# Retention and SwiGLU on one core: the first pair of heads by 128 tokens, products of the identity ahead of it, a new order of the first loads, and keys of pairs five to eight loaded once

## The chip, the core and the metric

The kernel runs on one core of a Trainium2 chip. The time is in device microseconds (us), from the start of the program on the core to its end; smaller is better. A "profiled execution" is one execution that the hardware profiler recorded; its span is what the trace covers, and its own time is what the same clock as in the timed runs gave for it.

The engines are TensorE (PE; its weight loads are listed apart as PEld), VectorE (DVE), ScalarE (ACT), GpSimd (POOL) and SyncE (SP), which here only issues transfers. Sixteen DMA engines move the data.

## The reference

```python
# attention: q, k, v are (8 batches, 8 heads, 576 tokens, 64) in float32
scores = scale * q @ k.T                       # scale = 1 / sqrt(64)
gamma  = 1 - 2 ** (-5 - head)
ret    = scores * where(i >= j, gamma ** (i - j), 0)     # i: query, j: key
attn   = ret @ v
# bridge: (8, 8, 576, 64) -> x of (4608 tokens, 512)
# feed-forward: the three weights are float64
g   = x @ w_gate                               # (512, 1536)
val = x @ w_val                                # (512, 1536)
out = (g * sigmoid(g) * val) @ w_out           # (1536, 512)
```

The result is float32, 4608 by 512.

## The kernel before

**Retention.** Two heads make a pair, and each batch has four pairs, so there are 32 pairs; the text counts them from 1, the code from 0 (`HP` is 4, so pairs 1 to 4 are `i < HP`, the first batch). A pair's 576 tokens are nine chunks of 64. Inside a chunk the scores are computed and masked (scores, L573; mask `near`, L580); from chunk to chunk a 64x64 state is carried: `new_states` (L543) multiplies scaled keys by values, and the states of the chunks are summed with decays on VectorE: pairs of chunks (L596), odd chunks (L603), even chunks (L608), after ScalarE has copied the even states out of PSUM (`copies`, L584). `own_values` (L532) multiplies values by the masked scores; `earlier_values` (L559) adds queries times states; `to_x` (L640 and L645) copies the sum into `x`, the input of the feed-forward part. On the first four pairs only eight of the nine chunks are done; the ninth chunks of the four pairs are done together later (`end_loads`, `end_scores` and the others with `end_`).

Queries and keys are needed with the head's dimension on the partitions. In the first four pairs TensorE transposes them (L466), four 128x128 blocks each, into PSUM, and ScalarE (VectorE for pair 1) copies them to `qT` and `kT` (L470 to L473). From pair 5 on, q and k come by columns in four transfers each (L282) into 32-row strips, and one 32x32 transposition by VectorE (L492) finishes the work; k is loaded a second time by tokens (L287 to L291) for the states. Keys are scaled in `keys` (L505 or L507); queries of pairs 2 to 4 by GpSimd in `scale_run` (L735).

**Feed-forward.** The first 512 tokens are computed plainly: for each of twelve hidden blocks of 128, `up0` (L842 to L857) adds four 512-column products (one for each 128 rows of `x`, "input blocks", that is, for each pair) for the gate and four for the value, ScalarE takes silu (L856), VectorE multiplies (L857); then `down0` (L864) adds four 512-column products for each hidden block. Hidden blocks use the banks A and B, or C and E, in turn. The rest of the tokens go through a scheme with fewer products (L1186, L1392), with sums of operands on VectorE and GpSimd; it fills the time after 172 us.

**Weights.** They come as float64 and are made float32 in the kernel: `load_w` brings 256 columns, 1 MB (for the first four transfers' worth as four pieces of 256 KB each, L370; later in one transfer), ScalarE splits the bits of a half (`split`, L389 and L390) and VectorE rounds and packs them (`rounding`, L406 and L407). The first five transfers are issued on SyncE, the later ones on ScalarE. A raw buffer is free when its two halves have been split, and `split` then issues the next load; the fifth load is held until a fixed place.

**Order.** On the five engines the order of the instructions is that of the program (`manual_schedule`, L1425). The first batch is written as six calls of `tick(t, 0, HP)` (L1427): each brings transposes of pair t, scores and states of the pair before, and own and earlier values of the pair before that. TensorE's sequence from 20 us on is: transposes of pair 4, own and earlier values of pair 3, hidden block 0 with input blocks 0 and 1 (four products), scores and states of pair 4, hidden block 1 with input blocks 0 and 1, own and earlier values of pair 4, and then hidden blocks 0 and 1 with input blocks 2 and 3 (L1434). After that a `plan` (L1450 to L1480) mixes the hidden blocks 2 to 11 with the rounding of weights (`round_until`), loads of pairs, and the ticks of pairs 5 to 10: `tick(4)` stands ahead of hidden block 2, `tick(5)` behind block 3, and the next ones behind blocks 5, 7, 10 and 11. The pieces of a tick on VectorE, ScalarE and GpSimd are put in a list, `pieces`, and drained by `go_on`.

SyncE issues, in order: the small part of a table of decays (`tab[:, 0:NCOL]`, L311), q, k and v of pairs 1 and 2 (shared with ScalarE), pair 3, the large part of the table (L337), pair 4, then the first two weights' pieces, the third and the fourth, each in 256 KB pieces; pair 5 and the fifth weight follow from within the ticks.

## Time and profile before

| | |
|---|---|
| timed runs | 1015.04, 1016.25, 1018.67 us; median 1016.25 |
| profiled execution, its own time | 1014.55 us |
| its span in the trace | 1012.8 us |
| TensorE busy in the span | 1000.9 us (99%) |
| VectorE, GpSimd, ScalarE busy | 710.9, 561.8, 286.7 us |
| moved by DMA | 194.38 MB in 278,892 packets |
| end of TensorE's last product | 1009.4 us |
| first transpose of pair 4 on TensorE | 20.54 us |
| hidden blocks 0 and 1 begin their third input block | 33.98 us |
| end of the plain down products, about | 172 us |

All times of the trace are counted from the start of the span. A group in the timeline is a run of like instructions without a gap: start, busy time, engine, line, operation, out and in, shape and count; in brackets the engine's idle time before it and what ended that. One float32 product or transpose of 128 columns or more can appear as two records, and some records are missing, so counts are not exact. Busy times in the listings include the overlap of neighbouring instructions; the step from one start to the next is the price of one in a dense sequence.

### The profile page before, as it was taken

How to read it: one execution, taken by the hardware profiler on the slowest of the kernel's cores; microseconds unless marked ns; L12 is line 12 of the kernel's file. 1: busy time of each engine (PE TensorE's matmuls, PEld its weight loads, DVE VectorE, ACT ScalarE, POOL GpSimd, SP SyncE). 2: the span in 40 equal slices, each digit the busy share in tenths (PEclk: the TensorE clock that was granted, in tenths of full speed). 3: DMA queues.
4: the chain of work that ended last, by engine and by line, in shares of the span. 5: the costliest groups of instructions: out<-in, count | busy, mean ns of one | idle time of the engine just before them, and what ended most of it. 6: DMA issues, size and time to landing. Idle time of an engine off the chain costs nothing.

```text
span 1012.8 us, 21319 instructions
## 1 busy us (share of the span) xinstructions
PE 1000.9 (99%) x8336; PEld 825.5 (82%) x8336; DVE 710.9 (70%) x1206; ACT 286.7 (28%) x636; POOL 561.8 (55%) x589
## 2 busy tenths in 40 slices
PE   6999999999999999999999999999999999999998
PEld 5655555888888888888888888888888888888887
DVE  4488887677875766977777678866575767566645
ACT  4565522132423312133422202233220012232110
POOL 3400359979375228575564157746672586566514
PEclk9999999999999999999999999999999999999999
DMA  9999866967587787647677777434454554445553
GB/s 245 261 288 272 192 216 234 264 193 214 138 238 207 217 231 193 198 156 196 184 202 206 198 179 217 154 133 159 161 172 141 154 189 147 148 155 180 182 159 102
DMA packets 278892, 194.38 MB, mean 192 GB/s; under 512 B 212552, under 2 KB 246088, under 8 KB 278792
## 3 DMA queue, kind: packets, MB, share of 16 engines
q1 hardware_dynamic: 251464, 94.70, 36.7%
q10 hardware_dynamic: 26688, 97.92, 29.1%
q8 instruction: 66, 1.08, 0.5%
q0 software_dynamic: 640, 0.39, 0.2%
q14 instruction: 34, 0.28, 0.1%
HBM read 154.04 MB, written 38.93 MB: 191 GB/s over the span
## 4 chain that ended last, share of the span: by engine, by line
PE 94%; DVE 2%; DMA 1%; POOL 1%; SPq 0%; issue 0%; ACT 0%; DVEq 0%; ACTq 0%; POOLq 0%
PE bankB L1186 12%; PE bankC L1186 11%; PE bankA L1186 11%; PE bankE L1186 11%; PE bankB L1392 7%; PE bankC L1392 7%; PE bankE L1392 6%; PE bankA L1392 6%; PE outer L532 2%; PE bankE L853 2%; PE bankA L853 2%; PE outer L1186 2%; PE inner L1186 2%; PE bankB L853 2%; PE outer L559 2%; PE bankC L853 2%
## 5 line engine op out<-in xcount | busy, mean ns | idle before, releaser
L1042 POOL TENSOR_TENSOR rest<-rest 128x512 f32<-128x512 f32 (+1 forms) x139 | 148.0, 1076 | 159.9 <-DVE rest L1042 112.5
L1201 POOL TENSOR_TENSOR arena<-rest,io 128x256 f32<-128x256 f32 x168 | 123.9, 750 | 89.4 <-ACT io L1200 88.9
L1200 ACT ACTIVATE io<-rest 128x256 f32<-128x256 f32 x192 | 79.3, 417 | 200.0 <-DVE rest L1042 140.0
L1186 PE MATMUL bankB<-rest,arena 128*128 128x256 f32 x448 | 114.5, 380 | 0.0
L1042 DVE TENSOR_TENSOR rest<-bankB,rest 128x512 f32<-128x512 f32 x116 | 78.5, 685 | 40.5 <-PE bankB L1186 28.5
L1186 PE MATMUL bankC<-rest,arena 128*128 128x256 f32 x416 | 106.3, 380 | 0.0
L1186 PE MATMUL bankA<-rest,arena 128*128 128x256 f32 x412 | 104.8, 379 | 0.0
L1042 DVE TENSOR_TENSOR rest<-bankA,rest 128x512 f32<-128x512 f32 x111 | 75.2, 685 | 40.8 <-PE bankA L1186 19.3
L1042 DVE TENSOR_TENSOR rest<-bankC,rest 128x512 f32<-128x512 f32 x110 | 74.5, 683 | 38.0 <-PE bankC L1186 23.4
L1042 DVE TENSOR_TENSOR rest<-bankE,rest 128x512 f32<-128x512 f32 x106 | 71.7, 684 | 36.2 <-PE bankE L1186 17.6
L1186 PE MATMUL bankE<-rest,arena 128*128 128x256 f32 x372 | 94.9, 380 | 0.3 <-DVE rest L1042 0.3
L1186 PEld LDWEIGHTS bankB<-rest,arena 128*128 128x128 f32 x448 | 84.7, 190 | 11.9 <-DVE rest L1042 0.2
L1186 PEld LDWEIGHTS bankC<-rest,arena 128*128 128x128 f32 x416 | 78.5, 190 | 11.4 <-DVE rest L1042 0.8
L1186 PEld LDWEIGHTS bankA<-rest,arena 128*128 128x128 f32 x412 | 78.1, 190 | 10.9 <-DVE rest L1042 0.2
L1186 PEld LDWEIGHTS bankE<-rest,arena 128*128 128x128 f32 x372 | 70.3, 190 | 10.4 <-DVE rest L1042 0.8
L1042 POOL TENSOR_TENSOR arena<-arena 128x256 f32<-128x256 f32 (+1 forms) x76 | 70.3, 947 | 11.1 <-PE bankC L1186 9.0
L886 POOL TENSOR_TENSOR rest<-rest 128x512 f32<-128x512 f32 x21 | 28.5, 1377 | 72.1 <-DVE rest L407 58.5
L1392 PE MATMUL bankB<-arena 128*128 128x256 f32 x264 | 61.0, 381 | 0.0
L1392 PE MATMUL bankE<-arena 128*128 128x256 f32 x264 | 60.8, 380 | 0.0
L1392 PEld LDWEIGHTS bankE<-arena 128*128 128x128 f32 x264 | 50.0, 190 | 6.9
L1392 PEld LDWEIGHTS bankB<-arena 128*128 128x128 f32 x264 | 49.8, 190 | 6.9
L1392 PE MATMUL bankC<-arena 128*128 128x256 f32 x240 | 55.2, 379 | 0.0
(270 smaller groups left out, 1876.0 us busy)
## 6 DMA issues: line engine op xcount, KB each, us to landing
arena<-up ACTq DMA_DIRECT2D x63, 896.0 KB, 4.6
arena<-dn ACTq DMA_DIRECT2D x65, 384.0 KB, 3.1
arena<-dn SPq DMA_DIRECT2D x39, 384.0 KB, 3.1
out_dram<-rest SPq DMA_DIRECT2D x31, 256.0 KB, 3.4
qk<-in_q_dram SPq DMA_DIRECT2D x108, 72.0 KB, 3.1
qk<-in_k_dram SPq DMA_DIRECT2D x108, 72.0 KB, 3.4
dn<-rest SPq DMA_DIRECT2D x26, 256.0 KB, 2.8
up<-arena SPq DMA_DIRECT2D x13, 512.0 KB, 5.6
```

Of the source, the lines that this page charges most:

```text
L532: m = nc.tensor.matmul(value(i, hl, c), s["v"][rows, at], ret[rows, c % 2 if whole(i) else hl, c // 2], start=start, stop=start, skip_grou ...
L559: nc.tensor.matmul(xr[half[hl]] if c + 1 == NC else value(i, hl, c), state[half[hl], c, :], s["qT"][half[hl], ts(c, L)], start=False, stop ...
L853: nc.tensor.matmul(bank, w, xs[0][:, c, :], start=(c == 0), stop=(c == HP - 1))
L886: eng.tensor_tensor(out=dst, in0=srcs[0], in1=srcs[1], op=ALU.add if op[0] == "add" else ALU.subtract)
L1042: eng.tensor_tensor(out=out, in0=a, in1=b, op=ALU.add if sign > 0 else ALU.subtract)
L1186: m = nc.tensor.matmul(b[:, g * TB : (g + 1) * TB], w[:, g], x, start=(opens and g == 0), stop=True, skip_group_check=True)
L1200: nc.scalar.activation(out=s, in_=src[:, 0:TB], func=AF.Silu)
L1201: (nc.vector if busy and o != 2 and qd + 1 < NQ else nc.gpsimd).tensor_tensor(out=hid[:, qd, 2 * H + h, 2 * T + t], in0=src[:, TB : 2 * TB ...
L1392: nc.tensor.matmul(b[:, m * TB : (m + 1) * TB], lhs[:, qd, ts(m, P)], w[:, qd], start=(opens and qd == 0 and m == 0), stop=(qd == NQ - 1), ...
```

## The change

**First pair.** The six ticks of the first batch are replaced by a sequence written out (`scale_run`, `first_scores`, `turn_pair`, ...). TensorE starts with two 64x64 and six 128x128 products of the identity into bank B, whose result nobody reads, and has two more behind the transposes of q and one behind those of k. Pair 1 works on blocks of 128 tokens instead of chunks of 64: eight scores of 128 columns, eight states, eight own values, six earlier values, with masks and tables of its own; its states are summed in a plain chain of blocks, without the even and odd steps. The query's scale is put in when `qT` is copied, so its result goes to `x` by one ScalarE copy.

```diff
+    def first_scores():
+        ...
+        for _ in range(2):
+            nc.tensor.matmul(bankB[0:D, 0:D], ident[0:D, 0:D], ident[0:D, 0:D], start=True, stop=True)
+        for src, bank, idle in ((None, None, 6), (qk, bankE, 2), (kn, bankC, 1)):
+            for c in range(NFULL if bank else 0):
+                nc.tensor.transpose(bank[:, ts(c, P)], src[:, ts(c, P)], ident)
+            for _ in range(idle):
+                nc.tensor.matmul(bankB[:, 0:P], ident, ident, start=True, stop=True)
+        ...
+        nc.vector.tensor_tensor(out=blocks(qT), in0=blocks(bankE), in1=table(first_qry), op=ALU.mult)
+        nc.vector.tensor_copy(kT[:, 0 : CW // 2], bankC[:, 0 : CW // 2])
+        nc.scalar.copy(kT[:, CW // 2 : CW], bankC[:, CW // 2 :])
+        ...
+        for c, hl in first:
+            nc.tensor.matmul(inner[:, hl, ts(c, P)], kT[half[hl], ts(c, P)], qT[half[hl], ts(c, P)],
+                             start=True, stop=True, skip_group_check=True)
+        for hl in range(2):
+            nc.vector.tensor_tensor(out=first_ret[:, hl], in0=blocks(inner[:, hl]), in1=table(first_near[:, ts(hl, P)]), op=ALU.mult)
+    def first_states():
+        ...
+            nc.tensor.matmul(sums[half[hl], c], s["kn"][:, head(c, hl)], s["v"][:, head(c, hl)],
                             start=True, stop=True, skip_group_check=True)
+        nc.vector.tensor_copy(state[:, 1], sums[:, 0])
+        for c in range(1, NFULL):
+            nc.vector.scalar_tensor_tensor(out=state[:, c + 1] if c + 1 < NFULL else end_states[:, 0], in0=state[:, c],
+                                           scalar=step[:, HP : HP + 1], in1=sums[:, c], op0=ALU.mult, op1=ALU.add)
+    def first_own():
+        ...
+            st[0]["own"] = nc.tensor.matmul(outer[half[hl], 0, ts(c, P)], st[0]["v"][:, head(c, hl)], first_ret[:, hl, c],
                                            start=(c == 0), stop=(c == 0), skip_group_check=True)
+    def first_out():
+        ...
+        for c, hl in first[2:]:
+            nc.tensor.matmul(outer[half[hl], 0, ts(c, P)], state[half[hl], c], s["qT"][half[hl], ts(c, P)],
                             start=False, stop=True, skip_group_check=True)
+        nc.scalar.copy(out=xs[0][:, 0], in_=outer[:, 0])
```

**Order of the start.** The two products of hidden block 0 with each of its first two inputs are spread between the steps of pairs 2 to 4 instead of standing in one row:

```diff
-    for t in range(HP + 2):
-        tick(t, 0, HP)
-        if t == 3:
-            load(HP)
-        for j in {3: (1,), 5: (4, 5)}.get(t, ()):
-            rounding(j)
+    scale_run(1)
+    first_scores()
+    scale_run(2)
+    turn_pair(1)
+    first_states()
+    first_own()
+    new_pair(1)
+    turn_pair(2)
+    first_out()
+    split(0)
+    rounding(0, False)
+    scale_run(3)
+    new_pair(2)
+    own_values(1)
+    split(1)
+    up0(0, [0], [0])
+    earlier_values(1)
+    to_x(1)[0]()
+    put = transposes(3)
+    rounding(1, False)
+    for f in put:
+        f()
+    up0(0, [1], [0])
+    up0(0, [0], [1])
+    split(2)
+    own_values(2)
+    earlier_values(2)
+    up0(0, [1], [1])
+    to_x(2)[0]()
+    rounding(2)
+    rounding(3, False)
+    new_pair(3)
+    while held:
+        held.pop()()
+    load(HP)
+    nc.sync.dma_start(out=tab[:, NCOL:], in_=decays[:, NCOL:])
+    split(4)
+    up0(1, range(2))
+    own_values(3)
+    earlier_values(3)
+    to_x(3)[0]()
+    for j in (4, 5):
+        rounding(j)
```

**Loads.** q of pair 1 goes out first, the small table (now with pair 1's tables) behind pair 1's q and k; the values of pairs 1 and 2 follow after the keys of both. The first half of the first two weights goes ahead of pair 4, the second half behind it; the third and the fourth weight are one transfer each; pair 5 follows the fifth weight; the large part of the table comes after pair 5:

```diff
-    for f in range(2):
-        for m in range(2):
-            load_w(m, (f,))
+    for m in range(2):
+        load_w(m, (0,))
+    load(3)()
+    for m in range(2):
+        load_w(m, (1,))
     load_w(2)
     load_w(3)
...
-            for cols in [ts(2 * f + n, D) for f in parts for n in range(2)] if m <= RAWS else [slice(0, 2 * P)]:
+            for cols in [ts(2 * f + n, D) for f in parts for n in range(2)] if m < 2 else [slice(0, 2 * P)]:
```

**Pairs 5 to 8.** k and v are loaded by tokens once (`natural`), each head on its own 64 rows. The keys' transposes are made on the chip by `turn_keys`; the chunks of the second parity lie on the other half of the rows, so the mask takes three instructions instead of one, and the even states two copies instead of one. Their tick places `turn_keys` as a piece of its own, ahead of the masks; `tick(4)` moves from ahead of hidden block 2 to behind it.

```diff
-            for n, src in enumerate((q, k)):
+            for n, src in enumerate((q,) if natural(i) else (q, k)):
...
+        def turn_keys():
+            kept = qk[:, 1, 0:NC]
+            at = kT.rearrange("p (c x t) -> p c x t", x=2, t=SQ)
+            nc.vector.transpose(out=kT, in_=kn)
+            nc.gpsimd.tensor_copy(out=kept, in_=at[:, :, 1])
+            for lo in (0, D):
+                one, two = slice(lo, lo + SQ), slice(lo + SQ, lo + D)
+                nc.scalar.copy(out=at[one, :, 1], in_=at[two, :, 0])
+                nc.scalar.copy(out=at[two, :, 0], in_=kept[one])
+            nc.scalar.activation(out=kn[:, 0:CW], in_=kn[:, 0:CW], func=AF.Copy, scale=own_key[:, p : p + 1])
...
+            if natural(i):
+                for rows, to, x in [(every, every, 0)] + [(*e, 1) for e in exchanged]:
+                    nc.vector.tensor_tensor(out=ret[to, x], in0=sc[rows, x], in1=near[rows, 2 * p + x].unsqueeze(1).to_broadcast(list(sc[rows, x].shape)),
                                            op=ALU.mult)
+                return
...
+            if natural(i):
+                for rows, to in exchanged:
+                    nc.scalar.copy(out=even[to], in_=z[rows, 1])
+                return
...
-    plan.insert(1, lambda: tick(HP, HP, FIRST))
...
+        if f == 3:
+            plan.append(lambda: tick(HP, HP, FIRST))
```

## The prediction

> **What bounds the kernel now.** I read the page's engine line first, then TensorE's waits, its timeline up to 35 us, the stretches, and last the trace's DMA completions and semaphore events, which tell for every product how long its operands had been ready.
>
> The engine line of the page, and what TensorE waited for (us in all, times, longest):
>
> ```profile
> PE 1000.9 (99%) x8336; PEld 825.5 (82%) x8336; DVE 710.9 (70%) x1206; ACT 286.7 (28%) x636; POOL 561.8 (55%) x589
> ```
>
> ```profile
> PE bankA L466 <- DMA qk<-in_q_dram: 4.6, 1, 4.6
> PE outer L532 <- ACT rest L389: 1.0, 1, 1.0
> PE inner L573 <- ACT rest L470: 0.7, 1, 0.7
> PE inner L573 <- DVE kT L472: 0.5, 1, 0.5
> PE bankB L466 <- DMA kn<-in_k_dram: 0.3, 1, 0.3
> PE bankE L1186 <- DVE rest L1042: 0.3, 1, 0.3
> ```
>
> TensorE is the bound: all its idle time is 8.5 us inside its work and 3.4 us behind its last product, and 7.8 us of it lie before 34 us. Whatever arrives earlier at 34 us should arrive earlier at the end. TensorE's timeline (start, us, group, idle before):
>
> ```profile
> 4.63 1.09 PE L466 MATMUL bankA<-ident,qk 128*128 128x128 f32 x4 [4.63 <-DMA qk<-in_q_dram]
> 9.67 1.12 PE L466 MATMUL bankB<-ident,kn 128*128 128x128 f32 x4
> 16.03 1.06 PE L466 MATMUL bankA<-ident,rest 128*128 128x128 f32 x4
> 20.54 0.66 PE L466 MATMUL bankC<-ident,rest 128*128 128x128 f32 x4
> 24.11 1.98 PE L853 MATMUL bankA<-rest,arena 128*128 128x512 f32 x4
> 27.74 0.69 PE L573 MATMUL inner<-rest,kT 64*64 64x64 f32 x32
> 33.98 1.12 PE L853 MATMUL bankA<-rest,arena 128*128 128x512 f32 x2
> ```
>
> Four transposes step at 0.21 us each up to 16.9 us and at 0.11 us at 20.5 us: the array runs at half pace until about 17.1 us, though the column of the granted clock says 1.00. So there are two things to win before 34 us: waits, and half pace. My yardstick is the group at 33.98, where the third input block of hidden blocks 0 and 1 begins; from there on the old and the new order of TensorE agree in cost. Stretches (length; busy PE, PEld, DVE, ACT, POOL; clock; DMA share; GB/s):
>
> ```profile
> 4.60:17.10 12.50, 10.88 (x188) 9.10 (x192) 6.25 (x16) 5.17 (x10) 3.89 (x4) 1.00 1.23 259
> 34.00:112.00 78.00, 78.00 (x688) 42.91 (x690) 56.39 (x116) 47.55 (x85) 10.17 (x17) 1.00 1.05 270
> 112.00:172.00 60.00, 59.91 (x760) 31.29 (x754) 53.81 (x93) 18.16 (x51) 40.79 (x32) 1.00 0.76 224
> ```
>
> The DMA engines are full from the first load to 112 us.
>
> **The change, part by part.**
>
> *Identity products.* The identity is written at 1.50 us (GpSimd), so TensorE begins at about 1.6 instead of 4.63. A transpose is one pass of 0.21; a product shows two records, so 0.43 at 128 and 0.21 at 64 columns: 2 x 0.21 + 6 x 0.43 = 3.0, to 4.6. q of pair 1 now goes out first (the table went ahead of it on SyncE, 0.4 us; q landed at 4.50), and is there. Then q's transposes 0.9, two products 0.85, k's transposes 0.9, one product 0.43: 7.7, and with the copy of kT (0.42) the scores begin at 7.9, against 7.62. Nothing is won by then. But TensorE is dense from 1.6 to 7.7, where before it had gaps of 0.3, 0.5 and 0.7 up to 12.4, and full pace came only at 17.1, after 4.7 dense us. I take full pace from about 7 to 8.5.
>
> *First pair by 128 tokens.* Scores 8 products of 128 columns on half the rows, states 8 of 64, own 8 of 128, earlier 6 of 128. If two run beside each other, as four 64x64 do now (16 take 0.5 at full pace, 32 ns each), that is 0.85 + 0.43 + 0.85 + 0.64 = 2.8; if not, 5.5; before, 3.5 at half pace. I take 2.8, the nearest row being that of the 64x64 tiles. VectorE loses one pairing chain and gains a second mask (0.7): level.
>
> *The path to pair 4.* From 7.9, at full pace: scores 0.85, transposes of pair 2 0.93, states 0.43, own 0.85, scores and states of pair 2 1.1, transposes of pair 3 0.93, earlier values 0.64, scores and states of pair 3 1.1, own values of pair 2 0.5, one hidden product 0.9, earlier values 0.6: 8.8. Waits on the way: v of pair 1 lands near 9.5 (0.6), the mask (0.2), copies and GpSimd's scaling of pair 3 (0.5), the rounding of the first weight half behind ScalarE's copy (0.8): TensorE is ready for pair 4's transposes near 18.2 to 18.8.
>
> *Order of the loads.* Here is the new bound. k of pair 4 landed at 15.45 before; now four weight pieces (256 KB, 0.84 us each by their landings) go ahead of it, and the second table (0.7) no longer does; the first has grown (0.25): 15.45 - 0.7 + 0.25 + 3.4 = 18.4. A 16 KB instruction fetch sat on one DMA engine for 1.3 us at 15.1, and the landings behind it came 1.4 late; later ones cost 0 to 0.6. So 18.4 to 19.8, and I take 19.0. Half-pace losses, tiles that do not overlap, and the 0.8 us stall are hidden behind this up to some 0.8 us.
>
> *From there to the yardstick.* Transposes 0.93, two hidden products 1.72, own and earlier values of pair 3 1.58, one hidden product 0.96, scores and states 1.21, four hidden products 3.63, own and earlier values 1.49: 11.5, all from the rows between 20.5 and 33.98 without their waits. The weight halves they need land by 24.2 (their rounding ends near 27.2, needed at 27.3 to 27.9). So the yardstick stands at 30.5 instead of 33.98: 3.4 us earlier.
>
> *Third and fourth weight in one transfer each; k once.* Between 30 and 110 us the SyncE queue held 53% of 16 engines for 40807 packets, 16.6 ns each. k by columns is 2304 packets a pair: 2.4 us, 9.6 us for four pairs, no longer moved. The weights, 4096 packets at about 30 ns, become 1024: 0 to 1.8 us less. None of it is on TensorE's path (the weight rounding came 1.4 to 8 us ahead of its product), so I cost it at nothing; it pays for the 3.4 us that TensorE now runs ahead. If that cover fails, TensorE waits for a weight up to those 3.4 us.
>
> *k transposed on chip, pairs 5 to 8.* A VectorE transpose as before (0.77), a GpSimd copy of 288 columns (0.4 to 1.0, by its copies of 256 and 512), four ScalarE copies on 32 rows (0.27 to 0.4 each), a scaling (0.6), two half copies of the even states instead of one (+0.2), three masks instead of one (1.27 against 0.69). The turned keys are needed 7 to 17 us later. VectorE idles 21.6 us between 34 and 112, which hides the chain; if it does not, the third rival has the price. Pair 8's two added masks are not hidden: from its outputs at 112.14 on VectorE has no rest until the down products, slowed from 117.7 to 123.7 beside GpSimd's additions (1.5 us for a rounding step of 0.7):
>
> ```profile
> 122.19 1.54 DVE L407 CUSTOM_DVE_ANT_0 rest<-rest 128x1024 uint16<-128x1024 uint16 x1
> 123.66 0.68 DVE L857 TENSOR_TENSOR arena<-bankE,io 128x512 f32<-128x512 f32 x1
> ```
>
> ```profile
> 124.48 1.03 PE L864 MATMUL bankE<-rest,arena 128*128 128x512 f32 x2
> ```
>
> That multiplication frees bankE at 124.34, for the product at 124.48: 0.14 to spare, against 0.6 more work. So 0 (the slow stretch gives it back) to 0.46; I take 0.2.
>
> **The sum.** 3.4 - 0.2 = 3.2 us off the profiled execution's own 1014.55, its span of 1012.8 falling to 1009.6. The median of the three runs, 1016.25, stands 1.7 above that execution; I carry the difference over: 1013.0. The bounds: k landing at 18.4 or 19.8, the overlap of tiles (if absent, 2.7 more on the way to pair 4, 1.9 of it past the cover) and the masks give a gain of 2.2 to 4.4 in most combinations.
>
> A rule of the skill speaks against the early full pace. The trace first: the eight transposes from 15.12 to 16.9 stood directly ahead of the change of pace, so transposes did not hold it back here. The Trainium skill, page "TensorE: Matmul & The Clock Gate", Part 4: PE-mode transpose, says that a transpose does not count as busy time for the clock gate the way a product does. By that rule the identity products, 3.0 us with eight transposes among them, would not be enough, and the first rival below is what would come.
>
> **The rivals.**
> 1. *Half pace stays until about 15.* For it: the 16 transposes and the first pair's products between 4.63 and 12.4 did not bring full pace, with gaps of under 0.8. Against it: the gaps are gone now, and after the last one it took 4.7 us. At half pace the 8.8 us of work become up to 15; with full pace from 14 TensorE reaches pair 4 at about 21.4 instead of 19.0. Gain 3.2 - 2.4 = 0.8: 1015.4. Chance 0.18.
> 2. *More is won.* The instruction fetch misses pair 4's loads, k lands at 18.2 to 18.4 and TensorE is there: 0.8 more; and the fuller first 30 us no longer cost the timed runs their surplus of 1.7, which I think sits in early transfers. Gain 4.3 to 6: about 1011. Chance 0.13.
> 3. *Slower: the key chain holds VectorE and ScalarE.* At pairs 6 to 8 the mask waits behind the new transpose, and for ScalarE's even copies, which now stand behind four copies that wait for GpSimd: 0.77 + 1.0 + 1.4 + 0.6 + 0.5 = 4.3 us a pair in which VectorE rounds no weight and ScalarE splits none and issues no weight transfer. Three times is 12.9. The halves come 6 to 9 us ahead of use in blocks 6 to 11; past 6, the rest (6.9) is on TensorE: 6.9 - 3.2 = 3.7 slower, 1020. It decides once these stalls sum to more than 6 + 3.2. Against it: between pairs VectorE has idle time to catch up (1.1 in 80 to 85, 1.8 in 85 to 90), the outputs of the pair before (1.5) fill part of the wait, and the four pairs no longer move 9.6 us of small packets ahead of the weights. Chance 0.14.
> 4. *It does nothing.* Pair 4's k lands at 22, behind the weights and further traffic, and TensorE waits there for all that it gained: 1016. For it: the engines are full in these stretches. Against it: the bytes ahead of k come to 19.0. Chance 0.03.
>
> **How the numbers follow.** About 0.3%, 3.05 us, is what a measurement of this kernel can tell from no change: faster is below 1013.2. The forecast has 0.52: 0.40 of it beyond that bound, as its centre is just past it and its upper bounds reach further than its lower, and 0.12 within. Faster 0.40 + 0.13 = 0.53; the same 0.12 + 0.18 + 0.03 = 0.33; slower 0.14. The forecast's own range is 1011.8 to 1014.1. The range for 8 in 10 takes in rivals 1 and 4 and half of 2, and leaves out most of 3: 1010.4 to 1017.4.
>
> **What would show it.** Right: TensorE's first product at about 1.6; transposes stepping at 0.11 us from pair 2 on (before, from pair 4 on); the longest wait inside its work ahead of pair 4's transposes, for a DMA of k; the third input block (the product of hidden blocks 0 and 1 that stood at 33.98) at about 30.5; and from there the same distances to the end, but for up to 0.5 at the first down products, waiting for VectorE. Wrong: pair 2's transposes at 0.21 (rival 1); k landing after 20.5; TensorE waiting for a rounding or for turned keys between 31 and 112 us, with VectorE's masks held by ScalarE (rival 3); a first pair whose 128-wide products step one behind the other.

## The result, and the profile after

| | before | after |
|---|---|---|
| median of the timed runs | 1017.17 us (4 runs) | 1027.83 us (4 runs, 1027.16 to 1028.38) |
| ratio | | 1.0104, 95% interval 1.0087 to 1.0120 |
| profiled execution, its own time | 1014.55 us | 1027.87 us |
| its span | 1012.8 us | 1026.2 us |

The changed kernel is about 1% slower: 10.7 us by the medians, 13.4 us between the two profiled executions. The forecast was 1013.0 us, and its range ended at 1017.4.

The engine line of the page after, and two of TensorE's waits (us in all, times, longest):

```profile
PE 1007.6 (98%) x8294; PEld 829.7 (81%) x8294; DVE 714.4 (70%) x1212; ACT 294.7 (29%) x652; POOL 563.6 (55%) x594
```

```profile
PE bankA L914 <- ACT io L917: 6.5, 2, 5.3
PE inner L589 <- issue: 3.0, 1, 3.0
```

TensorE's busy time grew by 6.7 us although the trace has slightly fewer of its records (8294 against 8336), so part of the loss is slow work and not waiting; and there is a wait that the page before did not have: 3 us for "issue", time for which the profile shows no releaser. TensorE's timeline after (start, us, group; in brackets the idle time before it):

```profile
18.09 1.12 PE L914 MATMUL bankA<-rest,arena 128*128 128x512 f32 x2 [1.62 <-DVE arena L429]
31.87 1.13 PE L914 MATMUL bankA<-rest,arena 128*128 128x512 f32 x2
...
39.97 3.72 PE L911 MATMUL bankA<-rest,arena 128*128 128x256 f32 x16 [0.96 <-ACT io L917]
89.84 3.70 PE L914 MATMUL bankA<-rest,arena 128*128 128x512 f32 x8 [1.14 <-ACT io L917]
100.24 3.60 PE L914 MATMUL bankE<-rest,arena 128*128 128x512 f32 x8
109.19 6.46 PE L914 MATMUL bankA<-rest,arena 128*128 128x512 f32 x8 [5.35 <-ACT io L917]
115.48 3.60 PE L914 MATMUL bankB<-rest,arena 128*128 128x512 f32 x8
...
628.69 0.57 PE L589 MATMUL inner<-qT,kT 64*64 64x64 f32 x21 [3.05 <-issue]
630.15 1.87 PE L1247 MATMUL bankB<-x_odd,arena 128*128 128x256 f32 x4
```

The third input block of hidden blocks 0 and 1 begins at 31.87 instead of 33.98, so the start did win 2.1 us. Then it waits three times for silu (L917, on ScalarE), for 0.96, 1.14 and 5.35 us. The eight records from 109.19 take 6.29 us to the next group, where groups of the same eight step at 3.43 otherwise (as from 96.81 to 100.24): after the long wait TensorE ran at half pace, which costs 2.86 more. Ahead of 628.69 it stops in the middle of a batch of scores, and two groups behind run at half pace again (1.87 and 1.91 for four records, 1.03 otherwise). The profile's granted clock shows both (the figure behind the busy times of the five engines; 1.00 is full):

```profile
107.95:114.77 6.82, 5.58 (x7) 2.49 (x8) 5.67 (x10) 5.78 (x11) 1.38 (x1) 0.50 1.01 323
630.19:633.60 3.41, 3.41 (x10) 2.69 (x9) 2.69 (x6) 0.34 (x1) 0.00 (x0) 0.50 0.32 113
```

The account between the two profiled executions, on TensorE: 2.11 won up to input block 3; 0.96 + 1.14 + 5.35 waiting and 2.86 at half pace, 10.31 in all, lost up to 116 us. That makes a net loss of 8.2; the first product of the scheme with fewer products begins at 181.01 against 172.19, 8.8 later, so 0.6 of that stretch is not itemised. From there to the last group the kernel before takes 835.75, the changed one 840.35: 4.6 more, which the stop (3.05) and its half pace (1.65) explain. 8.8 + 4.6 = 13.4.

Where the wait of 5.35 comes from is read on the two engines behind it. VectorE after, the masks of the two ticks before, and the stretch around the tick beside hidden block 7:

```profile
60.41 1.29 DVE L598 TENSOR_TENSOR ret<-inner,near 128x256 f32<-128x256 f32 x3 [3.93 <-ACT even L607]
79.33 1.30 DVE L598 TENSOR_TENSOR ret<-inner,near 128x256 f32<-128x256 f32 x3 [2.60 <-ACT even L607]
...
93.75 0.77 DVE L497 STREAM_TRANSPOSE kT<-kn 128x576 f32<-128x576 f32 x1
98.80 1.30 DVE L598 TENSOR_TENSOR ret<-inner,near 128x256 f32<-128x256 f32 x3 [2.96 <-ACT even L607]
103.81 0.43 DVE L428 TENSOR_SCALAR arena<-rest 128x512 int32<-128x512 int32 x1
```

and ScalarE in the same time:

```profile
95.46 0.43 ACT L501 COPY kT<-kT 32x288 f32<-32x288 f32 x1 [2.35 <-POOL qk L498]
98.02 0.74 ACT L607 COPY even<-inner 64x256 f32<-64x256 f32 x2
104.27 0.68 ACT L411 ACTIVATE rest<-rest 128x512 f32<-128x512 f32 x1 [4.37 <-DVE arena L428]
108.54 0.60 ACT L917 ACTIVATE io<-bankA 128x512 f32<-128x512 f32 x1
```

The mask of the last tick (L598, at 98.80) had its scores at 88.7, but VectorE stands 2.96 us for ScalarE's copies of the even states (L607). These stand behind the four copies of the turned keys (the first at 95.46), which wait for GpSimd, which waits for VectorE's transposition at 93.75. When the mask and the states are through, VectorE rounds again, from 103.81; only then is a buffer free for ScalarE's next split, at 104.27 after 4.4 us of nothing. Five more instructions and a DMA issue, and then silu, at 108.54. TensorE needs that silu to reuse bank A. In the two ticks before this one the masks waited 3.93 and 2.60 in the same way, and TensorE waited 1.14 for silu at 89.84. One stretch of the table by stages (length; busy PE, PEld, DVE, ACT, POOL; clock; DMA share; GB/s) sums it up:

```profile
34.00:112.00 78.00, 70.55 (x556) 38.32 (x555) 52.01 (x113) 47.50 (x87) 8.68 (x17) 0.97 0.97 230
```

VectorE is busy for 52.0 of these 78 us, less than the 56.4 before. It was not overloaded; it stood still for others.

### The profile page after: what moved, and what is told of

Same layout as the page of the kernel before. It is cut to its first block, busy times and chain, and to the rows that moved or that the text cites. A ratio compares the mean times of both kernels' runs of the same rounds, so it can differ in the third digit from the quotient of the medians.

```text
span 1026.2 us, 21259 instructions
## 1 busy us (share of the span) xinstructions
PE 1007.6 (98%) x8294; PEld 829.7 (81%) x8294; DVE 714.4 (70%) x1212; ACT 294.7 (29%) x652; POOL 563.6 (55%) x594
## 4 chain that ended last, share of the span: by engine, by line
PE 88%; DMA 4%; DVE 3%; SPq 2%; ACT 2%; issue 1%; ACTq 0%; POOL 0%; DVEq 0%; POOLq 0%
PE bankB L1247 12%; PE bankC L1247 12%; PE bankA L1247 11%; PE bankE L1247 11%; PE bankB L1453 7%; PE bankE L1453 7%; PE bankC L1453 7%; PE bankA L1453 6%; DMA rest<-in_moe_w_gate_dram 2%; PE inner L1247 2%; PE outer L1247 2%; PE outer L546 2%; PE inner L589 1%; PE outer L574 1%; PE inner L557 1%; PE bankA L925 1%
## 5 line engine op out<-in xcount | busy, mean ns | idle before, releaser
L1453 PE MATMUL bankA<-arena 128*128 128x256 f32 x228 | 52.5, 380 | 0.0
```

Source lines behind the costliest of these rows:

```text
L1453: nc.tensor.matmul(b[:, m * TB : (m + 1) * TB], lhs[:, qd, ts(m, P)], w[:, qd], start=(opens and qd == 0 and m == 0), stop=(qd == NQ - 1), ...
```

## The experiments

Times are medians of the runs that are compared; "before" is the kernel before on the same chip beside each experiment, 1016.0 to 1016.6. The ratios come from all runs of both kernels and not from the two medians, so they can differ from the quotient of the medians by 0.2%. Waits and starts come from one profiled execution of each kernel.

### k loaded twice again

```diff
     def natural(i):
-        return HP <= i < 2 * HP
+        return False
     def whole(i):
-        return 2 * HP <= i < needed(2) - 2
+        return HP <= i < needed(2) - 2
```

> The changed kernel with k of pairs 5 to 8 loaded twice again, by columns and by tokens, as before (its new start, load order and the later place of pair 5's tick stay). Theory A, the key chain: in the changed kernel VectorE's masks waited 3.9, 2.6 and 3.0 us for ScalarE's even copies, which stood behind the copies of the turned keys; the lag reached TensorE as waits of 1.1 and 5.4 us for silu, and as 2.9 us of half pace behind the second. Without the chain these 9.4 us should be gone: hidden blocks 0 and 1 begin input block 3 at about 31.9 as in the changed kernel, no wait of over 1 us behind them to 172 us, and 1013 to 1015 us if the 3 us stop at 628 us (with 1.7 of half pace) is gone too, 1018 to 1020 if it stays. Theory B, the order of the loads: the weights come later since pair 4 and the fifth weight go first, ScalarE's splits wait for them and silu behind them: the waits stay, 1025 to 1030 us, worse for the added bytes.

Measured: 1021.19 us, ratio 1.0048 (1.0033 to 1.0063). Input block 3 begins at 31.90. The waits for silu beside blocks 8 to 10 are gone, and the down part is over at 175.91 instead of 181.01: theory A holds, theory B does not. The time lies 1.2 us above the 1018 to 1020 that theory A gave with the stop, since two waits remain:

```profile
40.60 3.72 PE L910 MATMUL bankA<-rest,arena 128*128 128x256 f32 x16 [1.57 <-ACT io L916]
126.39 1.12 PE L924 MATMUL bankE<-rest,arena 128*128 128x512 f32 x2 [1.98 <-DVE arena L917]
```

The first was there in the changed kernel (0.96), the second is the one that the prediction had sized at 0 to 0.46: bank E for the fourth down product. It costs 2.0 even with the old masks, and 3.4 us at half clock behind it (127.55 to 130.96). It is VectorE that is late, and not TensorE that is early: the first down product begins at 121.56, only 0.25 ahead of the kernel before (121.81), but the multiplication that frees bank E ends at 126.33 instead of 124.34. It stands behind a silu that ScalarE finished at 111.1 instead of 107.0; ahead of that, ScalarE's scaling of keys had waited 5.7 and 5.8 us for k by tokens, and a split 1.56 us for a weight. How much of the delay each of these makes was not tested. The stop near 623 us is there, with 1.68.

### The kernel before with k loaded once

Only the parts of the change that concern pairs 5 to 8, on the kernel before: one load of k and v, `turn_keys`, three masks, and `tick(4)` behind block 2.

> The kernel before with only this part of the change: k and v of pairs 5 to 8 loaded once by token, keys turned on the chip, and pair 5's tick behind hidden block 2. Theory A: TensorE waits for silu in blocks 8 to 10 as in the changed kernel, 5 to 9 us: 1021 to 1026 us. Theory B: with the old order of loads nothing waits, and 9.6 us of small packets fewer: 1015 to 1018 us.

Measured: 1032.51 us, ratio 1.0156 (1.0128 to 1.0185), slower than either theory said.

```profile
63.37 1.19 PE L572 MATMUL inner<-v,kn 64*64 64x64 f32 x30 [8.13 <-ACT kn L518]
101.45 3.70 PE L898 MATMUL bankA<-rest,arena 128*128 128x512 f32 x8 [1.36 <-ACT io L901]
120.44 5.38 PE L898 MATMUL bankA<-rest,arena 128*128 128x512 f32 x6 [4.99 <-ACT io L901]
```

The last two lines are the signature of the changed kernel (1.14 and 5.35 there), and the masks waited 3.93, 2.61 and 2.60 us for the even copies as they did there (3.93, 2.60, 2.96): the chain brings it along without the new start. The first line is this kernel's own: ScalarE had waited 11.9 us for the fifth weight behind pair 5's load, so the keys of pair 5, behind that weight's splits, came 8.1 us late; the half clock behind that wait lasted until 67.55. In the changed kernel the fifth weight goes first, and there is no such wait.

### The turned keys behind the masks

```diff
-            pieces.append(keys)
+            new = [keys] + new
             keys = lambda: None
```

> The changed kernel with one piece moved: the turning of the keys (the transpose, GpSimd's copy, ScalarE's four copies and the scaling) stands behind the masks and states of its tick instead of ahead of them. Theory A: the masks wait no longer, VectorE gains 2 to 3 us in each of three ticks, and the waits for silu of 1.1 and 5.4 us shrink to under 1 in all: 1016 to 1021 us. If the mere amount of work on VectorE and ScalarE is what is late and not the wait, 1024 to 1028 us. Theory B: unchanged, 1027 to 1028 us.

Measured: 1026.57 us, ratio 1.0119 (1.0078 to 1.0161). The masks wait no longer, and yet TensorE waits 2.04 and 5.43 us for silu. ScalarE's timeline says why:

```profile
101.03 0.43 ACT L501 COPY kT<-kT 32x288 f32<-32x288 f32 x1 [6.46 <-POOL qk L498]
```

The stand has moved from VectorE to ScalarE: it waits 6.46 us for GpSimd's copy, since the transposition ahead of that copy now stands behind the whole mask and state work, and the splits and silu stand behind it. (Input block 3 begins at 32.81 here, 0.9 later than in the changed kernel: behind the wait of 1.63 us for the first rounding the granted clock was 0.50 from 18.6 to 22.0. There is no wait at 40 us.)

### Without the products of the identity

```diff
-        for _ in range(2):
-            nc.tensor.matmul(bankB[0:D, 0:D], ident[0:D, 0:D], ident[0:D, 0:D], start=True, stop=True)
-        for src, bank, idle in ((None, None, 6), (qk, bankE, 2), (kn, bankC, 1)):
+        for src, bank, idle in ((qk, bankE, 0), (kn, bankC, 0)):
```

> The changed kernel without the nine leading products of the identity (six, two and one of 128 columns and the two of 64). If they bring the early full pace, as the prediction had it: the transposes of pair 2 step at 0.21 us instead of 0.11, full pace comes between 12 and 17 us, hidden blocks 0 and 1 begin input block 3 later by 1 to 2.5 us than 31.87, and the time is 1028 to 1030 us. If pair 4's loads hide it all: 31.9 and 1027.8 us.

Measured: 1030.16 us, ratio 1.0136 (1.0102 to 1.0170).

```profile
9.54 1.11 PE L479 MATMUL bankC<-ident,kn 128*128 128x128 f32 x4
19.54 0.68 PE L546 MATMUL outer<-rest,v 64*64 64x64 f32 x27 [1.24 <-issue]
```

Pair 2's first four transposes step at 0.22 us (9.54 to 10.44), where the changed kernel has 0.12 (8.85 to 9.34), and the granted clock is full from 13.29 instead of 5.55. So the products do bring the early pace. At input block 3 they are worth 1.8 us (33.69 against 31.87), of which 1.24 is a stop of the kind treated below, so 0.6 without it. Most of what they win is hidden, at 18.09, by the wait for the rounding of the first weight: it takes 1.62 us there, and this kernel has no such wait.

### The even copies ahead of the turned keys

```diff
         if lo <= t < hi and natural(t):
+            pieces.append(copies)
+            copies = lambda: None
             pieces.append(keys)
```

> The changed kernel with one piece moved: ScalarE's copies of the even states stand ahead of the turning of the keys instead of behind it; VectorE's key transpose still stands ahead of the masks. If the order within the chain is what cost the 9.4 us (masks waiting 2.6 to 3.9 us for copies that stand behind GpSimd's copy and four copies on ScalarE): the masks wait under 1 us, ScalarE turns the keys while VectorE masks and sums, in the 4.4 us in which it waited for VectorE anyway, and the waits for silu of 1.1 and 5.4 us fall to under 1 together: 1016 to 1020 us with the stop of 3 us at 628 us still there. If any added work on ScalarE and VectorE comes late, as moving the whole chain behind the masks suggests (it moved the stand from VectorE to ScalarE, waits 2.0 and 5.4): 1024 to 1027 us.

Measured: 1017.22 us, ratio 1.0017 (1.0001 to 1.0032); its ten runs lie between 1016.6 and 1023.0. VectorE beside block 7:

```profile
90.18 0.78 DVE L497 STREAM_TRANSPOSE kT<-kn 128x576 f32<-128x576 f32 x1 [0.73 <-PE inner L589]
92.28 1.30 DVE L598 TENSOR_TENSOR ret<-inner,near 128x256 f32<-128x256 f32 x3
```

The mask no longer waits for ScalarE, which copies the even states while VectorE transposes, and turns the keys while VectorE masks: the order within the chain was the cause, not the amount of work. The down part is over at 172.77 against 181.01. On TensorE there remain a wait of 2.13 us for silu ahead of 41.32 and the stop:

```profile
618.79 0.57 PE L589 MATMUL inner<-qT,kT 64*64 64x64 f32 x21 [1.68 <-issue]
```

This moves one piece of the changed kernel and takes off 10 of its 11 us. Between the profiled executions 8.2 us of that are won by the end of the down part; the rest, 1.7, is a shorter stop (1.68 instead of 3.05), which the edit does not explain. It does not beat the kernel before.

### Pair 5 ahead of the fifth weight

```diff
+    load(HP)
+    nc.sync.dma_start(out=tab[:, NCOL:], in_=decays[:, NCOL:])
     while held:
         held.pop()()
-    load(HP)
-    nc.sync.dma_start(out=tab[:, NCOL:], in_=decays[:, NCOL:])
```

> As the kernel with the even copies first, and also the load of pair 5 and the table ahead of the fifth weight on SyncE, as before the change. If the wait of 1 us at 40 us (silu behind the split of a weight that landed at 38.1) comes from this order, it goes, and the time is about 1 us under the kernel with the even copies first; if the fifth weight is then late instead, a wait of 1 to 3 us near 48 us takes its place.

Measured: 1019.16 us, ratio 1.0025 (1.0006 to 1.0044). The wait at 40 us goes, as expected, but the time is not lower: the product into bank E at the fourth down product now waits 2.90 us for VectorE, and there is a stop of 2.24 at 622 us. VectorE itself is late again: its multiplication ends at 126.72, against 124.91 with the even copies first, behind splits on ScalarE that waited 2.5 and 2.4 us for weights to land. The eight runs spread from 1014.0 to 1021.8, and the profiled one took 1021.64, so these waits are those of one of the longest.

### Empty instructions

> The changed kernel with 100 empty instructions on TensorE ahead of the first hidden product, where it waits 1.6 us for VectorE anyway; nothing else differs. They shift every later instruction by 100 places. The stop of 3.0 us that the trace calls issue stood at the 3270th to 3275th instruction of TensorE's stream in four kernels, among them the one without identity products, whose stream is 11 shorter. If it belongs to the place in the stream (a fetch of code that comes late there), it now stands 100 instructions earlier in the work, ahead of the tick at 624 us, or is gone since 256-column products take longer to run than code to arrive: up to 4.7 us less behind 600 us. If it belongs to the work (scores of that tick, with its loads), it stays at the same scores.

The 100 empty instructions are not in the compiled program, so these are further runs of the changed kernel: 1027.32 us, waits for silu of 0.73, 1.58 and 5.34, and the stop at the same score, with 2.65. Two more stops show, of 0.77 at 16.4 and 0.39 at 297.1, which the first profile of the same program does not have. It says nothing on where the stop belongs.

### The new start alone

The kernel with k loaded twice again, with pair 5's load ahead of the fifth weight and `tick(4)` ahead of block 2, as before the change.

> The new start alone: the first pair by 128 tokens, the identity products, the new order of loads up to the fourth weight; pairs 5 to 8 with k loaded twice, pair 5's load ahead of the fifth weight and its tick ahead of hidden block 2, as before the change. If what is won at the start reaches the end, input block 3 begins at about 31.9 (2.1 earlier than before) and the time is 1013.5 to 1015 us, or 4.7 more if the stop at 628 us comes with the new start. If VectorE and ScalarE cannot follow 2 us earlier, TensorE waits as much later on, at the latest at the product of the first down block that waited 2.0 for bank E with k loaded twice: 1016 to 1018 us, or 1021 with the stop.

Measured: 1019.74 us, ratio 1.0041 (1.0019 to 1.0062).

```profile
40.39 3.72 PE L910 MATMUL bankA<-rest,arena 128*128 128x256 f32 x16 [1.45 <-ACT io L916]
```

Input block 3 begins at 31.81, 2.2 us ahead of the kernel before. At 40.39 it gives back 1.45; the product that needs bank E starts at 124.03 (124.48 before) without a wait, and the down part ends at 171.83, 0.4 ahead. The rest is a stop of 3.12 at 619.74 with its half pace: from the end of the down part to the last group 841.0 us against 835.75. So the new start is worth 0.4 us at the end of the plain part, and the kernel that has it loses about 5 at the stop.

### A longer stream of instructions

```diff
+        for _ in range(54):
+            nc.tensor.matmul(bankB[0:D, 0:16], ident[0:D, 0:D], ident[0:D, 0:16], start=True, stop=True)
...
     split(1)
+    for _ in range(50):
+        nc.tensor.matmul(bankB[0:D, 0:16], ident[0:D, 0:D], ident[0:D, 0:16], start=True, stop=True)
     up0(0, [0], [0])
```

> The kernel with the even copies first, with 100 products more on TensorE: 54 small ones of the identity (16 columns) in place of four of its 128-column ones at the start, and 50 such ahead of the first hidden product, where TensorE waits 1.7 us for VectorE. (The 100 empty instructions asked for before had been dropped when that kernel was compiled, so it was a second run of the changed kernel: the stop stood at the same score.) If the stop at 619 us belongs to a place in the stream of instructions, it now stands 100 instructions earlier in the work, ahead of the tick, or is gone: 2 to 3 us less behind 600 us, 1014 to 1016 us. If it belongs to the work, it stays at the tenth score of that tick with 1.7 to 3 us, and the time stays at 1016 to 1018 us. The start may come 0 to 1 us later.

> As the kernel with 100 products more, and ScalarE issues the seventh weight's load behind the first two silu instead of ahead of the split before them. In the changed kernel this issue stood still from about 34 to 37.3 on ScalarE and the splits and silu behind it, and TensorE waited 1.0 us at 40 us (2.1 in the kernel with the even copies first). If that issue is what held silu: the wait at 40 us goes, and nothing else moves: 1 to 2 us less than the kernel with 100 products more. If VectorE's next roundings were the limit anyway, the wait turns up at the first down products (up to 2 us for bank E at 124 to 127 us) and the time is the same.

Measured: 1043.64 us (ratio 1.0259, 1.0230 to 1.0289) and 1042.64 us (1.0250, 1.0220 to 1.0280). The small products took 0.215 us each, as much as one of 64 columns, and put the first hidden product back by 21 us (39.55 in the first, against 18.50 with the even copies first; the expectation of the next experiments says 8), so these times tell nothing of the disputed waits. What they tell is where the stops stand: none in the tick beside 640 us, but four others, of 1.3 to 2.7 us, in each kernel at the same instructions (28.9, 114.9, 168.0 and 434.8 us in the first). And though the small products left no gap, they did not bring full pace: in the first kernel they run from 2.03 to 13.6 us and the granted clock is full only from 19.32, 5.7 us into the wider products and transposes; the second fifty run from 29.25 at 0.50, and it stays at 0.50 until 43.21.

### Shifts of 64 and of 32 products at no cost

```diff
-                if f == 2 or f == 3 and gv == 0:
+                if f == 2 or f == 3 and gv == 0 or 4 <= f < 12:     # 4 <= f < 8 in the second
...
-            if j == 3:
+            if j in (3, 5):
...
     for c in range(2, HP):
         for f in range(2):
             up0(f, [c])
+    while held:
+        held.pop()()
```

> The kernel with the even copies first, without added products, and two changes: ScalarE issues the seventh weight's load behind the first two silu, and hidden blocks 4 to 11 use products of 256 columns (two for each of 512), which costs TensorE 3.45 against 3.44 us for four by the rows of blocks 2 and 4 and shifts the later stream by 64 instructions. (The 100 small products of the last two kernels took 0.215 us each and put the start back by 8 us, so their times say nothing; the stop was gone from the tick's scores there and others stood at other work, which fits a place in the stream.) If the wait at 40 us comes from that issue: it goes (2.1 in the kernel with the even copies first), and the down part is reached by 171 to 172 us, against 172.8. If the stop is tied to the place in the stream, it leaves the tenth score of the tick at 619 us: 1012.5 to 1015 us without a stop, 1015 to 1017 us with one elsewhere. If VectorE cannot follow, bank E waits up to 2.9 us at 124 to 127: 1015 to 1017 us.

> The same with blocks 4 to 7 alone in products of 256 columns, a shift of 32 instructions. The start and the stretch to 172 us should be as in the kernel with a shift of 64; what differs is where a late fetch of code meets TensorE. If the stop is gone in both: equal times, 1012.5 to 1015 us. If in one alone: 2 to 4.7 us between them.

Measured: 1023.37 us (ratio 1.0079, 1.0061 to 1.0097) and 1020.11 us (1.0039, 1.0025 to 1.0052). Neither reached the time that was expected. The wait at 40 us is gone in both: ScalarE's issue of that load, which waited in front of the silu, was its cause. (The first kernel shows it best, since its input block 3 begins at 31.87 as in the changed kernel; in the second the clock was 0.50 from 18.97 to 22.39 and the block begins at 33.08.) But the down part ends at 179.0 and 178.4 instead of 171 to 172, for new stops ahead of it. Shifted by 64 products, the stop of the tick is again at the same score; others have come (another of 2.7 us at 99.0):

```profile
74.33 0.49 PE L729 MATMUL outer<-rest 64*64 64x64 f32 x7 [3.92 <-issue]
...
625.05 0.57 PE L589 MATMUL inner<-qT,kT 64*64 64x64 f32 x21 [1.40 <-issue]
```

Shifted by 32, the one in the tick is gone, and a single one remains, of 3.5 us at 75.5; bank E at the fourth down product waits 0.8.

So a shift of 64 products changes nothing for that stop, and a shift of 32 removes it: the place repeats with 64 products. In the trace a float32 product is two weight loads and two multiplications (a transpose is one of each), so 64 products are 256 instructions. I counted TensorE's records (multiplications, weight loads, semaphore waits) up to each stop for "issue" of over 0.3 us in the changed kernel and the twelve experiments: 28 stops, and all of them stand at a count of 193 or 194 beyond a multiple of 256. The kernel without identity products fits too: its stream is 11 products shorter, and its stop stands 11 products further on in the work, behind the tick's last score. The trace also has the transfers of code, 65 to 67 of them with 16,384 bytes each, as many as a program of that length has blocks of 256 instructions. In the changed kernel TensorE starts no product between 625.42 and 628.69; such a transfer begins at 626.22 and takes 1.06 us. In each of the 28 stops the next product begins 1.2 to 1.6 us behind the end of a transfer, and it is always the transfer whose number in the order is that of the block; no block in the 14 profiles is entered sooner than 1.2 us behind its own.

So the stop is a block of TensorE's code that comes late. The Trainium skill, page "Runtime: NRT & Kernel Launch", section "Instruction fetch mechanics", says that code is refilled in blocks of 16 KiB, 256 instructions, while the engine works on the block before, and that crossing a boundary is mostly hidden. The size and the period agree with these runs; that it is hidden holds for most boundaries, and not for these 28, which cost 0.4 to 3.9 us each and often half pace behind the longer ones. In the kernel before, the same boundary falls among the scores and states of the same tick at 615.9 us, and it is hidden since its transfer had ended at 602.2, 13.8 us ahead: that transfer began 2.5 us before TensorE entered the block in front, which took 12.6 us. In the changed kernel it began 5.6 us after TensorE had entered the block in front, which holds so many short products that it was through in 5. Why the transfer began so much later there was not found.

## Why the prediction was wrong, point by point

**The early full pace: right.** The identity products brought it by about 6 us (forecast: 7 to 8.5). The granted clock agrees, against what the prediction made of its column: full clock is recorded from 5.55 us on, and from 17.15 in the kernel before; the column showed 1.00 earlier than that because the trace has no clock record there. The first rival, half pace until about 15, did not come about; it came when the identity products were taken out (full clock at 13.3).

**The gain at the third input block: right in kind, too large.** 2.1 us instead of 3.4. The forecast had TensorE wait for pair 4's keys, landing at 19.0. Their transfers landed at 19.2 and 19.5, close to that, but TensorE was not there: it waited 1.62 us at 18.09 for the rounding of the first weight, a term that I had at 0.8 and called hidden, and began the transposes at 19.76. From there to input block 3 it took 12.1 us instead of 11.5. So 0.8 of the missing 1.4 lies ahead of the transposes, for the late rounding and the slightly later keys together, and 0.6 behind them.

**"None of it is on TensorE's path": wrong in part.** The one load in place of four did no harm of itself, but the order around it did: a load issued on ScalarE (37.27) waited there until the fifth weight, whose semaphore it uses, had landed (37.20), and silu behind it. That is 0.96 us at 40 us (1.5 to 2.1 in variants), and moving that issue removed it.

**"VectorE idles 21.6 us, which hides it": the step that failed.** It hid the chain's work under idle time, and so set one sum against another. What mattered is the order in each engine's queue: the masks waited for copies that stood behind a chain over three engines, 3.93, 2.60 and 2.96 us, 9.5 in all. The third rival named exactly this chain and priced its stalls at 12.9. It had the wrong cover: I let the delay first eat the 6 to 9 us by which weights are rounded ahead of use, but it reached TensorE through silu on ScalarE, which in the kernel before stood ready 2.5 us ahead of the product that needs bank A:

```profile
100.19 0.60 ACT L856 ACTIVATE io<-bankA 128x512 f32<-128x512 f32 x1
```

```profile
103.27 3.60 PE L853 MATMUL bankA<-rest,arena 128*128 128x512 f32 x8
```

I also left out that a wait of 5 us is followed by half pace, 2.9 us here. The rival got 0.14; by the queue order, visible in the program, it deserved to be the forecast.

**"From there on the old and the new order agree in cost": wrong.** The new start alone wins 2.2 us at input block 3 and has 0.4 left at 172 us. Of the loss 1.45 is the wait at 40 us for silu behind the issue on ScalarE: the transfer ahead of it could not come earlier as well. Bank E, the price that the prediction did set on this stretch, had 0.14 us to spare before; it cost nothing with the new start alone, and 2.0 and 2.9 in two variants in which ScalarE and with it VectorE came about 2 us later than before.

**The stop in the middle of the kernel: not foreseen at all.** 4.7 us with its half pace, in a tick that the change does not touch. Where a stop can stand is set by the length of the stream ahead of it; whether it does, by when the block of code was fetched.

By size, about: of 13.4 us, 9.4 are the waits for silu that the key chain causes with the half pace behind them, 1.0 the wait at 40 us, 4.7 the late code with its half pace and 0.6 not itemised, against 2.1 won.

## What to carry to other kernels

Work added to an idle engine is free only if nothing in its queue behind it is waited for: follow the added chain from engine to engine, and ask at each which instruction stands behind it and who needs that one. Here one line, the even copies ahead of the chain, took back 10 of 11 us, 8.2 of them by the end of the down part. And a stretch that is won at the start is worth at the end only what the next engine, or the next transfer, can come earlier by.

## What the runs showed of the hardware

- TensorE's code comes in blocks of 256 instructions, and a block can come late: 28 stops of 0.4 to 3.9 us, all at the same phase of 256 and all ended 1.2 to 1.6 us behind the end of a transfer of 16,384 bytes. Adding or removing products far ahead therefore moves, makes or removes a stop: 32 products more in hidden blocks 4 to 7 removed the one at 620 us. In the changed kernel the stop with its half pace cost 4.7 us. Which boundaries are late also varies between executions of one program (one stop in one profile, three in another).
- A long wait cost more than its length. With each of the ten waits and stops of 3 us or more after the first 20 us, the granted clock fell to 0.50 for 3.41, 6.83 or 10.24 us, once, twice or three times 3.41; eight records of the changed kernel took 6.29 us instead of 3.43 behind a wait of 5.35. Behind shorter waits it varied: half clock behind 1.68 us in one kernel (even copies first), none behind 2.90 in another (pair 5 first).
- A product of 16 columns took as long as one of 64 at half pace, 0.215 us, and ten microseconds of such products without a gap left the granted clock at 0.50.
